# Batch 0's start in a fused attention and maxout kernel: q packed on VectorE and turned in whole blocks, the second k half in two column tiles, two row sums ahead of the first weight

## The chip, the cores and the metric

The kernel runs on one core of one Trainium2 chip. The time is the device time of an execution in microseconds (us), given as the median of several runs. A profiled execution gives a page (busy times, chain of waits, groups of instructions) and a trace that can be asked for single stretches. Engines are named as the profile names them: PE is TensorE (PEld its weight loads), DVE is VectorE, ACT is ScalarE, POOL is GpSimd, and SP issues transfers.

## The reference

Two computations follow each other: a Linformer attention and a feed-forward block with a maximum over three projections. Batch 8, 8 heads, sequence 1024, head size 64; k and v are projected along the sequence to 64 rows each.

```python
k_proj = np.einsum('ks,bhsd->bhkd', E, k)
v_proj = np.einsum('ks,bhsd->bhkd', F, v)
scores = scale * np.matmul(q, k_proj.transpose(0, 1, 3, 2))
attn = np.exp(scores - np.max(scores, axis=-1, keepdims=True))
attn = attn / (np.sum(attn, axis=-1, keepdims=True) + 1e-09)
attn_out = np.matmul(attn, v_proj)
x = attn_out.transpose(0, 2, 1, 3).reshape(8192, 512)
h = np.maximum(np.maximum(x @ w1, x @ w2), x @ w3)      # 512 -> 768
out = h @ w_out                                         # 768 -> 512
```

All inputs and the output are float32.

## The kernel before

Everything is computed in bfloat16 with float32 sums. The order of the instructions on each engine is written out by hand; PSUM is one tile of eight banks, and a small model of the engines' times (`clock`, `free`) picks at build time the bank that it takes to be free first (`bank()`, or `two()` for a pair of banks). The calls `at(...)` and `pe(...)` only move that model's time and make no instruction.

Heads are worked on in pairs (four pairs, 0 to 3), since two heads of 64 fill 128 partitions. A half of the sequence is 512 rows, four blocks of 128. For a pair and a half, the steps are: q is turned so that its head dimension lies on the partitions (`qTs`); k is projected with E and turned (`kpTs`); v is projected with F (`vps`); `scores` multiplies the turned q and k; `exps` takes the exponential on ScalarE; `sums` (called by `z(g)`) multiplies the exponentials by ones, and `invert` takes logarithm and exponential of the negative on ScalarE to get the reciprocal; `values` (called by `x(g)`) multiplies by v, and `scale_x` multiplies by the reciprocals on VectorE and writes xT, the input of the feed-forward block. The maximum of the scores is not subtracted.

Batch 0 has no earlier work to hide behind, so its start has code of its own, line by line in the order in which it stands:

- POOL issues all loads in one order, each casting to bfloat16: the first q half of heads 0 to 3, k of heads 0 to 3, the same of heads 4 to 7, v of pairs 0 and 1, two strips of w1, v of pairs 2 and 3, two more strips of w1, w2, w3 and the second q half, then `w_out` and batch 1. Up to eight are under way; a further one waits for the landing of the one eight places before.
- `turn_ef` turns E and F. `q_duo(u)` turns q of pairs 2u and 2u+1: 16 transposes of 128x64, straight from the loaded tile, whose two heads lie apart, into two row halves of a bank (`heads_q`), and one copy out on VectorE.
- `k_duo(u)` projects k of four heads in 8 matmuls of 256 columns with 64 output rows; `kt_duo(u)` turns the result in two transposes.
- `v_pair(g)` projects v of one pair in 8 matmuls.
- `idle(n)` issues matmuls on zeros, which keep TensorE busy while it waits for loads.
- After the hand-written sequence, `up_first` does the feed-forward matmuls of batch 0's first half. For w1 it runs over strips `ct` (128 rows of w1, so one pair of heads) and blocks `jt` (128 of the 768 columns): strip 0 and 1 for blocks 0 to 3, strip 0 and 1 for blocks 4 and 5, then strips 2 and 3. The rest of the attention is hung between these matmuls by a key (weight, strip, block), after which it runs. w2 and w3 follow, and in between the second half's q is packed on ScalarE (`pack_q`) and turned in 128x128 blocks (`qp`).

Later batches have their attention placed between the feed-forward matmuls of the batch before (`plan`).

Of the kernel before, what the change touches and what calls it, by code (L numbers as in the profile page):

```python
# [9 lines left out]
BF16 = mybir.dt.bfloat16  # L10
# [5 lines left out]
def kernel(  # L16
# [65 lines left out]
    def bank():  # L82
        n = min(range(8), key=lambda n: free[n])
        deal((n,))
        return psum_t[:, n, :], (n,)

    def pe(dt, wait=0.0):
        clock["pe"] = max(clock["pe"], wait) + dt
        return clock["pe"]
# [122 lines left out]
    def scores(b, g, lo, nsi):  # L212
        t, ns = two()
        n = nsi // 2
        for c in range(2):
            for hp in range(2):
                rows = slice(hp * HALF, (hp + 1) * HALF)
                at = g * SI + lo + c * n
                nc.tensor.matmul(  # L219
                    out=t[c * HALF:(c + 1) * HALF, hp, 0:n * P],  # L220
                    lhsT=k_pair(b, g)[rows],
                    rhs=qTs[b][rows, at:at + n, :],
                    start=True, stop=True,
                )
        return t[:, :, 0:n * P], ns, pe(n * MM / 4 + 0.1)

    def exps(b, g, lo, nsi, sc):
        t, ns, ready = sc
        pTs[b, g, lo] = att.tile([P, 2, CHUNK], BF16, name="pT", bufs=6)[:, :, 0:nsi * HALF]
        nc.scalar.activation(out=pTs[b, g, lo], in_=t, func=AF.Exp, scale=scale)  # L230
        runs("s", ready, 0.17 + nsi * 0.107, ns)
# [126 lines left out]
                )  # L358
        pe(8 * (width * 0.00042 + 0.01))

    def heads_q(b, g, sis, t):
        for i, si in enumerate(sis):
            for hp in range(2):
                nc.tensor.transpose(
                    out=t[hp * HALF:(hp + 1) * HALF, i * P:(i + 1) * P],
                    in_=qkv[b][0][:, 2 * g + hp, si, :],
                    identity=ident,
                )
        pe(0.08 * len(sis))

    q_pk = {}

    def pack_q(b, gs, lo, nsi):


        def f():
            if b not in q_pk:
                q_pk[b] = att.tile([P, NPAIR, SI, 2, D], BF16, name="q_p", bufs=1)
            for g in gs:
                copy(  # L380
                    "s", q_pk[b][:, g, lo:lo + nsi].rearrange("p si h d -> p h si d"),
                    qkv[b][0][:, 2 * g:2 * g + 2, lo:lo + nsi], (), 0.58,
                )
        return f
# [178 lines left out]
    def idle(n, w=warm):  # L563

        t, ns = bank()
        for _ in range(n):
            nc.tensor.matmul(out=t, lhsT=w[:, 0:P], rhs=w, start=True, stop=True)  # L567
        free[ns[0]] = pe(n * MM * (4 if w is warm_f else 1))
# [19 lines left out]
    def at(us):  # L588
        clock["pe"] = max(clock["pe"], us)
# [3 lines left out]
    def k_duo(u):  # L593
        t, ns = bank()
        for si in range(SI):
            nc.tensor.matmul(
                out=t[0:KP, 0:4 * D], lhsT=efT[:, si, 0:KP],
                rhs=k_t[:, 4 * u:4 * u + 4, si, :],
                start=(si == 0), stop=(si == SI - 1),
            )  # L600
        pe(0.9)
        kp0[u] = att.tile([KP, 4 * D], BF16, name="kp0")
        copy("v", kp0[u], t[0:KP, 0:4 * D], ns, 0.45)

    def kt_duo(u):
        t, ns = bank()
        t = t.bitcast(BF16)
        for gg in range(2):
            nc.tensor.transpose(
                out=t[:, gg * KP:(gg + 1) * KP],  # L610
                in_=kp0[u][:, gg * P:(gg + 1) * P], identity=ident[0:KP, 0:KP],
            )
        pe(0.15)
        copy(
            "v", kpTs[0][:, 2 * u:2 * u + 2, :].rearrange("a g k -> a (g k)"),
            t[:, 0:2 * KP], ns, 0.25,
        )

    def v_pair(g):
        t, ns = bank()  # L620
        for si in range(SI):
            nc.tensor.matmul(
                out=t[:, 0:2 * D], lhsT=efT[:, si, KP:3 * KP],
                rhs=v_t[:, 2 * g:2 * g + 2, si, :],
                start=(si == 0), stop=(si == SI - 1),
            )
        pe(0.5)
        copy(
            "v", vps[0][:, 2 * g:2 * g + 2].rearrange("a h d -> a (h d)"),
            t[:, 0:2 * D], ns, 0.3,  # L630
        )

    def q_duo(u):
        t, ns = bank()
        t = t.bitcast(BF16)
        for gg in range(2):
            heads_q(0, 2 * u + gg, range(SPC), t[:, gg * CHUNK:(gg + 1) * CHUNK])
        o = qTs[0].rearrange("a (g si) p -> a g si p", si=SI)
        copy(
            "v", o[:, 2 * u:2 * u + 2, 0:SPC, :],  # L640
            t.rearrange("a (g si p) -> a g si p", si=SPC, p=P), ns, 0.7,
        )
# [3 lines left out]
    def z(g):  # L646
        invert(0, g, *C0, sums(0, g, *C0))

    def x(g):
        scale_x(0, g, *C0, values(0, g, *C0))  # L650
# [16 lines left out]
    z(0)  # L667
    idle(1)
    z(1)
    idle(1)  # L670
    at(12.8)
    k_duo(1)
    idle(1)
    at(14.8)
    v_pair(0)
    kt_duo(1)
    x(0)
    for g in (2, 3):
        exps(0, g, *C0, scores(0, g, *C0))
    at(16.1)  # L680
    v_pair(1)
    at(17.4)

    ffn_sb = ctx.enter_context(tc.tile_pool(name="ffn_sb", bufs=2))
    hTs = {}
# [205 lines left out]
    for b in range(B):  # L891
        p = plan(b)

        def behind(ch, step):
            for f in p.get((ch, step), []):
                f()

        for ch in range(NCHUNK):
            if (b, ch) == (0, 0):
                c1 = (SPC, SPC)  # L900
                up_first({
                    (0, 0, 1): [lambda: x(1)],
                    (0, 0, 3): [lambda: z(2), lambda: z(3)],
                    (0, 1, 1): [lambda: v_pair(2)],
                    (0, 1, 3): [lambda: x(2)],
                    (0, 1, 5): [lambda: v_pair(3), ld(1)],
                    (0, 2, 1): [lambda: x(3)],
                    (2, "a", 0): [pack_q(0, (0, 1), *c1)],
                    (2, "a", 1): [pack_q(0, (2, 3), *c1)],
                    (2, "a", 3): [qp(0, (0, 1), *c1)],  # L910
                    (2, "a", 5): [qp(0, (2, 3), *c1)],
                    (2, 1): [duo[0].scores],
                    (2, 4): [
                        duo[0].sums, duo[0].values, duo[1].scores, duo[0].invert,
                    ],
                })
                run_later()
                behind(0, NJT - 1)
            else:
                for step in range(NJT):  # L920
                    up(b, ch, step, lambda: behind(ch, (step, "mid")))
                    behind(ch, step)
            for tt in range(SPC):
                down(b, ch, tt, "v" if b == 0 else "s")
                behind(ch, NJT + tt)
# [30 lines left out]
```

## Time and profile before

| | us |
|---|---|
| median of 5 runs | 399.05 (398.83 to 399.52) |
| profiled execution | 399.06 |
| its span, first to last instruction | 397.3 |
| TensorE busy | 387.4 (98%) |
| VectorE busy | 202.3 (51%) |
| ScalarE busy | 152.1 (38%) |
| granted TensorE clock, mean | 0.998 |
| HBM traffic over the span | 218 GB/s |

The page lists busy time by engine, the span in 40 slices (a digit is a tenth of busy time), the chain of work that ended last (followed back from the last instruction, at each step to what released it), and groups of instructions with what ended the idle time ahead of them. Lines of the timeline give start and length in us, engine, line of the kernel, operation, and what is written from what; x8 at the end is a number of instructions merged into the line, and the bracket tells how long the engine was idle before and what released it. Matmuls overlap, so a group's length holds the tail of its last one. Of the changed part: L364 are the transposes of `heads_q`, L596 `k_duo`, L609 `kt_duo`, L622 `v_pair`, L219 `scores`, L230 `exps`, L239 `sums` and `values`, L299 and L305 `invert`, L316 `scale_x`, L689 the w1 to w3 matmuls, L393 the transposes of `qp`, L567 `idle`, L102 every plain copy.

### The profile page before, as it was taken

To read this page: it belongs to the slowest core of one execution; us is meant where nothing else is said; L and a number is where in the kernel's file an instruction comes from. 1 tells how busy PE (TensorE), PEld (TensorE's weight loads), DVE (VectorE), ACT (ScalarE), POOL (GpSimd) and SP (SyncE) were. 2 spreads that over 40 slices of the span, in tenths; PEclk is the share of its full clock that TensorE was granted. 3 is DMA by queue.
4 is the path that set the end of the run, shared out by engine and by line. 5 is a ranking of instruction groups with operands and counts; after the bars stand their busy time and mean duration, and the time that the engine had idled before them with its cause. 6 is when DMAs were issued, how large, how long until landed. Compare 5 with 4: busy or idle time off the path is not lost.

```text
span 397.3 us, 5598 instructions
## 1 busy us (share of the span) xinstructions
PE 387.4 (98%) x2196; PEld 173.5 (44%) x2238; DVE 202.3 (51%) x309; ACT 152.1 (38%) x236; POOL 34.5 (9%) x49
## 2 busy tenths in 40 slices
PE   7899999999999999999999999999999999999996
PEld 3544443453445445444444444444444444444443
DVE  3348756751764525645374544845266443745251
ACT  2534638527222552263323532245323533132322
POOL 7450001000400200200002000200000000000000
PEclk9999999999999999999999999999999999999999
DMA  9999999987999998999979979696971138020202
GB/s 151 206 205 207 205 232 154 244 160 159 230 182 265 153 221 201 227 179 210 209 207 149 245 164 273 98 243 117 222 206 42 64 86 237 2 106 0 107 0 106
DMA packets 67338, 66.29 MB, mean 167 GB/s; under 512 B 31504, under 2 KB 59792, under 8 KB 67312
## 3 DMA queue, kind: packets, MB, share of 16 engines
q0 software_dynamic: 29104, 30.41, 47.7%
q1 hardware_dynamic: 38064, 35.46, 34.7%
q8 instruction: 17, 0.28, 0.3%
q10 hardware_dynamic: 144, 0.07, 0.1%
q14 instruction: 9, 0.07, 0.1%
HBM read 69.73 MB, written 16.97 MB: 218 GB/s over the span
## 4 chain that ended last, share of the span: by engine, by line
PE 89%; DMA 3%; DVE 2%; ACT 2%; issue 2%; POOL 2%; DVEq 0%; ACTq 0%; POOLq 0%
PE banks L689 60%; PE banks L797 20%; DMA v_t<-in_v_dram 3%; PE banks L353 2%; PE banks L239 2%; PE banks L219 2%; PE banks L528 1%; PE banks L264 1%; DVE xT L316 1%; ACT zl L299 1%; DVE m L758 1%; ACT zi_all L305 1%; DVE hT L699 0%; POOL k_t L152 0%; POOL q_t L157 0%
## 5 line engine op out<-in xcount | busy, mean ns | idle before, releaser
L689 PE MATMUL banks<-xT,w_sb 128*128 128x512 bf16 x1125 | 255.2, 379 | 1.9 <-DVE xT L316 0.3
L689 PEld LDWEIGHTS <-w_sb 128*128 128x128 bf16 x1152 | 110.1, 98 | 136.7 <-issue 8.4
L758 DVE TENSOR_TENSOR m<-banks,h1s 128x512 f32<-128x512 f32 x90 | 62.1, 690 | 131.1 <-ACT h1s L754 88.5
L754 ACT COPY h1s<-banks 128x512 f32<-128x512 f32 x90 | 52.7, 586 | 119.5 <-PE banks L689 119.5
L797 PE MATMUL banks<-wout_sb,hT 128*128 128x512 bf16 x364 | 85.5, 379 | 1.0 <-issue 0.3
L699 DVE TENSOR_TENSOR hT<-banks,m 128x512 bf16<-128x512 f32 x90 | 62.3, 692 | 9.7 <-DVE m L758 0.5
L797 PEld LDWEIGHTS <-hT 128*128 128x128 bf16 x378 | 35.3, 98 | 48.4 <-issue 6.1
L102 ACT COPY o_sb<-banks 128x512 f32<-128x512 f32 (+2 forms) x57 | 32.9, 578 | 58.3 <-PE banks L797 50.6
L316 DVE TENSOR_TENSOR xT<-banks,zi_all 128x1024 bf16<-128x1024 f32 x28 | 33.2, 1220 | 12.8 <-PE banks L239 8.2
L230 ACT ACTIVATE pT<-banks 128x1024 bf16<-128x1024 f32 (+1 forms) x32 | 30.2, 975 | 15.9 <-PE banks L219 15.9
L201 POOL DMA_DIRECT2D q_t<-in_q_dram x7 | 6.2, 880 | 196.7 <-DMA qT<-q_p 85.0
L102 ACT CAST vp<-banks 64x256 bf16<-64x256 f32 (+1 forms) x11 | 4.7, 424 | 20.5 <-DVE kp L102 11.2
L102 DVE CAST vp<-banks 64x256 bf16<-64x256 f32 (+2 forms) x15 | 6.7, 444 | 10.1 <-ACT vp L102 7.3
L239 PE MATMUL banks<-pT,vp 64*64 64x512 bf16 (+1 forms) x128 | 10.3, 375 | 0.5 <-DVE vp L102 0.2
L102 DVE COPY q_p<-q_t 128x1024 bf16<-128x1024 bf16 x26 | 9.7, 434 | 0.4 <-DMA q_t<-in_q_dram 0.4
L219 PE MATMUL banks<-qT,kpT 64*64 64x512 bf16 (+1 forms) x128 | 9.7, 372 | 0.0
L102 DVE CAST kp<-banks 128x256 bf16<-128x256 f32 (+2 forms) x9 | 4.6, 509 | 8.5 <-PE banks L528 3.5
L102 DVE COPY o_sb<-banks 128x512 f32<-128x512 f32 (+1 forms) x9 | 5.6, 640 | 5.4 <-PE banks L777 4.5
L567 PE MATMUL banks<-warm_f 128*128 128x512 f32 x8 | 6.6, 971 | 1.5 <-DVE warm_f L175 1.5
L299 ACT ACTIVATE zl<-banks 128x512 f32<-128x512 f32 (+1 forms) x8 | 6.5, 811 | 2.9 <-PE banks L239 2.7
L353 PEld LDWEIGHTS <-efT 128*64 128x64 bf16 x128 | 6.6, 110 | 2.1 <-issue 2.1
L201 POOL DMA_DIRECT2D v_t<-in_v_dram x7 | 6.5, 930 | 1.0 <-PE banks L689 1.0
(76 smaller groups left out, 136.3 us busy)
## 6 DMA issues: line engine op xcount, KB each, us to landing
out_dram<-o_sb SPq DMA_DIRECT2D x30, 512.0 KB, 3.9
zi_all<-zd SPq DMA_DIRECT2D x20, 512.0 KB, 8.0
q_t<-in_q_dram POOLq DMA_DIRECT2D x7, 1024.0 KB, 10.2
k_t<-in_k_dram POOLq DMA_DIRECT2D x7, 1024.0 KB, 16.5
v_t<-in_v_dram POOLq DMA_DIRECT2D x7, 1024.0 KB, 21.5
zi_all<-zd POOLq DMA_DIRECT2D x4, 512.0 KB, 7.5
w_sb<-in_moe_w_dram POOLq DMA_DIRECT2D x4, 384.0 KB, 11.0
k_t<-in_k_dram POOLq DMA_DIRECT2D x2, 512.0 KB, 9.1
```

The lines of the kernel that those rows point to most:

```text
L102: done = {"v": nc.vector.tensor_copy, "s": nc.scalar.copy, "g": nc.gpsimd.tensor_copy}[eng](out=o, in_=i)
L201: dma = nc.gpsimd.dma_start(out=tiles[i], in_=view((q, k, v)[i], b))
L219: nc.tensor.matmul(out=t[c * HALF:(c + 1) * HALF, hp, 0:n * P], lhsT=k_pair(b, g)[rows], rhs=qTs[b][rows, at:at + n, :], start=True, stop= ...
L230: nc.scalar.activation(out=pTs[b, g, lo], in_=t, func=AF.Exp, scale=scale)
L239: nc.tensor.matmul(out=t[hp * HALF:(hp + 1) * HALF, c, 0:nsi * HALF], lhsT=w(rows, hp), rhs=p[rows, hp, :], start=True, stop=True,)
L316: nc.vector.tensor_tensor(out=xTs[b][:, g, lo:lo + nsi, :].rearrange("a (c s) p -> a c (s p)", c=2), in0=t, in1=zi, op=ALU.mult,)
L353: nc.tensor.matmul(out=t[hh * HALF:(hh + 1) * HALF, 0:width], lhsT=efT[:, si, (kv - 1) * KP:kv * KP], rhs=qkv[b][kv][:, heads[hh], si, :], ...
L689: nc.tensor.matmul(out=h, lhsT=w_sb[i][:, ct, jt * P:(jt + 1) * P], rhs=xTs[b][:, ct, ch * SPC:(ch + 1) * SPC, :], start=(ct == first), st ...
L699: nc.vector.tensor_tensor(out=o, in0=h, in1=other, op=ALU.max)
L754: nc.scalar.copy(out=h1s, in_=h[0][0])
L758: nc.vector.tensor_tensor(out=m12, in0=h[1][0], in1=h1s, op=ALU.max)
L797: nc.tensor.matmul(out=o_ps, lhsT=hTs[b, ch][:, jt, tt * P:(tt + 1) * P], rhs=wout_sb[:, jt, :], start=(jt == 0), stop=(jt == NJT - 1),)
```

## The change

Four things change, all in the start of batch 0; the loads and their order stay.

- `q_duo` first packs its pairs of q on VectorE (`pack_q`, which had ScalarE as its only engine), so that the two heads of a pair lie side by side, and turns 8 blocks of 128x128 in place of 16 of 128x64. `heads_q` goes.
- The second half of k is projected by `k_quad`: heads 4 and 5 into output rows 0 to 63, heads 6 and 7 into rows 64 to 127, as two column tiles of the array, 16 matmuls of 128 columns (`proj`, L353 before). `kt_quad` turns the result in one transpose. Two `idle(1)` go and one is moved.
- Scores of pairs 2 and 3 come ahead of `x(0)`, and their sums `z(2)`, `z(3)` ahead of the first w1 matmul; they stood behind w1's strip 0, block 3.
- `v_pair(2)` moves from behind strip 1, block 1 to behind strip 1, block 3, and `x(2)` from there to behind strip 0, block 5.

```diff
-    def heads_q(b, g, sis, t):
-        for i, si in enumerate(sis):
-            for hp in range(2):
-                nc.tensor.transpose(
-                    out=t[hp * HALF:(hp + 1) * HALF, i * P:(i + 1) * P],
-                    in_=qkv[b][0][:, 2 * g + hp, si, :],
-                    identity=ident,
-                )
-        pe(0.08 * len(sis))
...
-    def pack_q(b, gs, lo, nsi):
+    def pack_q(b, gs, lo, nsi, eng="s"):
...
                 copy(
-                    "s", q_pk[b][:, g, lo:lo + nsi].rearrange("p si h d -> p h si d"),
+                    eng, q_pk[b][:, g, lo:lo + nsi].rearrange("p si h d -> p h si d"),
...
+    def k_quad(u):
+
+        t, ns = bank()
+        proj(0, 1, t, (slice(4 * u, 4 * u + 2), slice(4 * u + 2, 4 * u + 4)), 2 * D)
+        kp0[u] = att.tile([P, 2 * D], BF16, name="kp0q", bufs=1)
+        copy("v", kp0[u], t[:, 0:2 * D], ns, 0.27)
+
+    def kt_quad(u):
+        t, ns = bank()
+        t = t.bitcast(BF16)
+        nc.tensor.transpose(out=t[:, 0:P], in_=kp0[u], identity=ident)
+        pe(0.1)
+        copy(
+            "v", kpTs[0][:, 2 * u:2 * u + 2, :].rearrange("a g k -> a (g k)"),
+            t[:, 0:P], ns, 0.25,
+        )
...
     def q_duo(u):
+        pack_q(0, (2 * u, 2 * u + 1), 0, SPC, "v")()
         t, ns = bank()
         t = t.bitcast(BF16)
         for gg in range(2):
-            heads_q(0, 2 * u + gg, range(SPC), t[:, gg * CHUNK:(gg + 1) * CHUNK])
+            for si in range(SPC):
+                at = (gg * SPC + si) * P
+                nc.tensor.transpose(
+                    out=t[:, at:at + P],
+                    in_=q_pk[0][:, 2 * u + gg, si].rearrange("p h d -> p (h d)"),
+                    identity=ident,
+                )
+        pe(0.5)
...
     z(1)
+    at(12.8)
+    k_quad(1)
     idle(1)
-    at(12.8)
-    k_duo(1)
-    idle(1)
+    kt_quad(1)
     at(14.8)
     v_pair(0)
-    kt_duo(1)
-    x(0)
     for g in (2, 3):
         exps(0, g, *C0, scores(0, g, *C0))
+    x(0)
     at(16.1)
     v_pair(1)
-    at(17.4)
+    z(2)
+    z(3)
+    at(17.0)
...
                     (0, 0, 1): [lambda: x(1)],
-                    (0, 0, 3): [lambda: z(2), lambda: z(3)],
-                    (0, 1, 1): [lambda: v_pair(2)],
-                    (0, 1, 3): [lambda: x(2)],
+                    (0, 1, 3): [lambda: v_pair(2)],
+                    (0, 0, 5): [lambda: x(2)],
                     (0, 1, 5): [lambda: v_pair(3), ld(1)],
```

## The prediction

> **What bounds the kernel now.** I read the page first, then the chain of waits, the waits of the start, and the timeline from 7 to 36 us.
>
> ```profile
> span 397.3 us, 5598 instructions
> PE 387.4 (98%) x2196; PEld 173.5 (44%) x2238; DVE 202.3 (51%) x309; ACT 152.1 (38%) x236; POOL 34.5 (9%) x49
> DMA  9999999987999998999979979696971138020202
> PE banks L689 60%; PE banks L797 20%; DMA v_t<-in_v_dram 3%; PE banks L353 2%; PE banks L239 2%; PE banks L219 2%; PE banks L528 1%; PE banks L264 1%; DVE xT L316 1%; ACT zl L299 1%; DVE m L758 1%; ACT zi_all L305 1%; DVE hT L699 0%; POOL k_t L152 0%; POOL q_t L157 0%
> ```
>
> TensorE is on the chain nearly everywhere, but the DMA row is full from the first slice, and the chain holds one transfer, v_t. The chain of the first 36 us in order of time shows where:
>
> ```profile
> 7.47 12.86 DMA v_t<-in_v_dram
> 20.33 0.05 issue
> 20.37 0.62 PE banks L622 x8
> 20.99 0.43 PE banks L689 x2
> 21.43 0.02 issue
> 21.45 0.30 PE banks L239 x4
> 21.75 0.97 PE banks L689 x4
> 22.72 0.50 PE banks L622 x8
> ```
>
> The third v transfer (pair 2) is issued at 7.47 and lands at 20.33; the projection of pair 2 (L622) starts 0.05 later. So before 20.33 TensorE cannot set the end, and what it does there is priced at nothing unless it is late for a landing. The landings, from the DMA view (issue plus time to landing): first q half 6.58, first k half 10.00, second q half 11.38, second k half 13.88, v pairs 0 and 1 at 15.16 and 16.45, w1's strips 17.43, 19.45, 22.56, 23.51, v pairs 2 and 3 at 20.33 and 21.65, w2 25.40 and 27.32, w3's first half 29.16, the q of sequence half 2 at 31.82, w3's second half 33.70. These issues wait only for earlier landings, the instruction order on POOL is unchanged, so the landings stay.
>
> After 20.33, in the timeline:
>
> ```profile
> 20.83 0.59 PE L689 MATMUL banks<-xT,w_sb 128*128 128x512 bf16 x2
> 21.10 0.29 DVE L102 CAST vp<-banks 128x128 bf16<-128x128 f32 x1 [1.74 <-PE banks L622]
> 21.45 0.30 PE L239 MATMUL banks<-pT,vp 64*64 64x256 bf16 x4
> 21.87 0.69 DVE L316 TENSOR_TENSOR xT<-banks,zi 128x512 bf16<-128x512 f32 x1 [0.48 <-PE banks L239]
> 22.61 0.61 PE L622 MATMUL banks<-v_t,efT 128*128 128x128 bf16 x8
> 31.84 2.18 ACT L102 COPY q_p<-q_t 128x512 bf16<-128x512 bf16 x4 [5.09 <-DMA q_t<-in_q_dram]
> ```
>
> The reader is to see a serial chain: project pair 2, cast it (VectorE), apply it, scale it (VectorE, until 22.56), and only then project pair 3 at 22.61. The four w1 matmuls before that end their issue at 22.55, so TensorE waits 0.06 for the scale, whose PSUM bank pair 3 reuses. The last line is the next DMA-bound point: ScalarE's packs of q start with their landing.
>
> **The change, part by part.** The profiled execution took 399.06 us (span 397.3, 1.76 around it), 0.01 over the median 399.05.
>
> First half of q, before k lands. Removed: 16 transposes and loads of 64 columns, 7.33 to 7.96 (issue 0.57 us). Added: two VectorE copies of 512 columns and 8 transposes of 128x128. A copy: the trace has 128x512 SBUF to SBUF at 0.283 (efT), 128x1024 at 0.42 (q_p); I take 0.28 with a start every 0.2, bounds 0.2 to 0.42. They stand behind VectorE's first efT copy (7.43 to 7.86) and end near 8.3. The transposes (0.056 apart in the q_p group on L393: 0.61 for 8) then end near 8.75, the following fp32 warm-up matmul (issue 1.12) near 9.8. The first k projection waits for its landing at 10.00 and starts at 10.04 in both: cover 0.24 us. What waits behind the copies on VectorE (the qT copy, 0.69, and the efT copy, 0.28) ends near 9.7, before its users at 12.13 and 15.2. Cost nothing.
>
> Second half of q. Its two copies follow the kpT copy (11.85 to 12.07) and end near 12.5; TensorE has scores until 12.47. The second four transposes start near 12.55 instead of 12.68, and the whole ends where it did, near 13.1, 0.05 either way. Sums of pair 0 wait for ScalarE's exponential (13.08) anyway. Cost nothing.
>
> A collision is possible in both places, since POOL issues transfers at 7.47 to 8.20 and 11.67 to 12.21. The trace has one q_p copy during such an issue:
>
> ```profile
> L102 DVE COPY q_p<-q_t x26: 407/421/791, 43.2 to 277.8; 128x1024 bf16<-128x1024 bf16 x26
> 103.12 1.15 POOL L201 DMA_DIRECT2D v_t<-in_v_dram  x1
> 86.43 0.88 POOL L201 DMA_DIRECT2D q_t<-in_q_dram  x1 [25.12 <-DMA qT<-q_p]
> ```
>
> The slowest copy (791 instead of 421 ns) started at 103.70, inside a POOL issue of 1.15 instead of 0.88. So a collision costs VectorE 0.37 and POOL 0.27. With 0.37 the first k projection would start 0.13 late (0.37 less its cover 0.24), and that is swallowed at 19.45 as below. The 0.27 at POOL falls on an issue whose transfer lands 12.86 later behind full queues: bounds 0 and 0.27 on the landing, I take 0 (DMA rates are 205 to 208 GB/s all through).
> The Trainium skill, "SBUF — State Buffer", section "Who interferes with whom", speaks against this part: a VectorE copy in a two-port mode shuts GpSimd out of SBUF for its whole length, and POOL-issued transfers need GpSimd for their descriptors. By that rule the sum would carry an estimate of 0.3 us on pair 2's landing, 399.3; by the rows it carries nothing.
>
> Second half of k. Removed: one 128x512 warm-up (0.22), 8 matmuls of 256 columns (14.24 to 15.30), a 64x256 cast of 0.416 that began at 15.41 because it waited for ScalarE, two 64-column transposes, one warm-up. Added: 16 matmuls of 128 columns in two column tiles, one cast 128x128 (0.29, the vp row), a warm-up, one transpose. The landing (13.88) releases it at 13.95. The row of L353, also two column tiles, has a pair each 0.109 at 256 columns; the 64-column q transposes have a pair each 0.053 at 128. I take 0.055: 8 pairs 0.44; upper bound 0.87, as if the shorter stream saved nothing. Cast 14.6 to 14.9, transpose to 15.15, kpT copy to 15.45. Scores 2, 3 then start after pair 0's projection (landing 15.16, issue 15.2 to 15.65) at 15.66 instead of 16.59. Their exponentials wait for ScalarE's inversion of pair 1 (ends 16.03) and run from 16.0 to 17.1 instead of 16.94 to 18.03. A gain of 0.93 locally.
>
> Pairs 2, 3's sums ahead of w1. They move from 19.01 to about 16.95 and 17.35; the latter waits for pair 0's scale, whose PSUM bank it takes. The first w1 matmul comes near 17.6 to 17.7 (before 17.72: its strip landed at 17.43). Then 2 w1, pair 1 applied, 2 more w1, done at 18.7. Here the gain ends: next in TensorE's order are four matmuls of w1's second strip, which lands at 19.45. TensorE stands about 0.8 us. So up to 0.8 us of lateness in all the steps above is free too.
>
> Pair 2's projection, now behind all four matmuls of the second strip (before: two, with two after). They start at 19.45 + 0.046 (landing to matmul, as 20.328 to 20.374 for v) = 19.49; 4 x 0.216 = 0.864 ends their issue at 20.36. Pair 2's landing releases it at 20.374. Cost: nothing, by a margin of 0.02 us. Its cast no longer waits for ScalarE as well: before it began 0.106 after the matmuls' end (20.994), other vp casts 0.04; gain 0.065. Apply at 21.38 (the two w1 matmuls ahead end at 21.26), scale ends 22.50, two w1 matmuls between, pair 3 at 22.55 instead of 22.61. TensorE now stands 0.4 us there, where it stood 0.06: the rest of the gain goes here.
>
> From there on the order on every engine is that of before, with the PSUM banks renamed throughout. The one added wait, batch 2's q load on VectorE's copies of 12.5, stands at 58.68 and is long fulfilled; SP's queue is unchanged. The strips of w1 (22.56, 23.51) and w2 (25.40; used from 26.07) lie earlier than their use.
>
> Sum: 399.06 - 0.065 + 0 = 399.0. Of roughly 1 us that TensorE saves, the landings and the scale give 0.065.
> The Trainium skill, "TensorEngine Tiling (Array Packing)", section "Restrictions", adds that column tiling turns fast weight loading off; the L353 loads (16 in 0.80) hold that in the upper bound of 0.87 already, and by the rule the sum would still be 399.0.
>
> **The rivals.** About 0.2%, 0.8 us, is what a measurement of this kernel tells from no change.
> A, slower: w1's second strip lands nearer to pair 2 than 0.88 us. Four matmuls now stand between that landing and pair 2's projection, so each 0.1 us closer costs 0.1. For it: the margin is 0.02, and neighbouring landings lie 0.88 to 2.02 apart. Against it: the issues are unchanged. Landing together costs 0.86: 399.06 - 0.065 + 0.86 = 399.85.
> B, more gain: the chain through pair 2 is shorter than I think, and TensorE reaches ScalarE's packs of q early. These follow the landing at 31.82: the second ends at 32.98, and the second four transposes, at 33.19 before, cannot start before 33.02. That caps the gain at 0.17: 398.9.
> C, slower: VectorE's copies, at 0.79 each, delay the first k projection by about 1 us (2 x 0.79 less 0.48 is 1.1 late, less the cover 0.24, so 0.86). The stand at 19.45 absorbs 0.8: 399.1. It decides only beyond 0.8.
> D, slower: TensorE's clock falls as it idles more. It stood 1.02 us before the first k projection and the granted clock read 1.00 after; the new stands are 0.8 and 0.4. Half clock for the 7 w1 matmuls or so of one stand would cost 7 x 0.216 = 1.5: 400.5.
>
> **How the numbers follow.** Forecast 0.72, B 0.10, A 0.11, C 0.04, D 0.03. The predicted time is 399.0. Low: the lowest run 398.83 less B's 0.17, rounded down, 398.6; high: A's end, 399.85. That leaves out D and part of the runs' own scatter (398.83 to 399.52). Beyond 0.8 us: slower D, a third of A, a little of C and 0.02 for causes that I do not see, 0.10; faster only by an unseen cause, since B is capped, 0.07; within, 0.83.
>
> **What would show it.** Right: scores of pairs 2, 3 near 15.7, TensorE standing before 19.45 and again before pair 3's projection, which starts at 22.5 to 22.6; the q_p transposes from 32.9. Wrong: pair 2's projection clearly after its landing (A), new VectorE copies above 0.5 us (C), w1 matmuls more than 0.216 apart (D), or landings that moved, above all those of w1's second strip and v pair 2.

## The result and the profile after

The changed kernel takes 399.69 us (median of 23 runs, 399.03 to 400.86), the kernel before 399.13 in the same comparison (42 runs, 398.57 to 399.95): ratio 1.0015, 95% interval 1.0009 to 1.0021. It is slower by 0.6 us. That lies inside the range given and under the 0.2% that I had named as the limit of what can be told, but so many runs tell more, and "no change" was the wrong call.

The profiled execution took 399.48 us. From its page, the span, TensorE's row, the DMA row of the 40 slices and the chain by line:

```profile
span 397.7 us, 5581 instructions
PE 386.5 (97%) x2186; PEld 173.2 (44%) x2228; DVE 203.0 (51%) x313; ACT 151.9 (38%) x236; POOL 34.2 (9%) x49
DMA  8999999988999999999978969796970138020202
PE banks L705 58%; PE banks L813 19%; DMA qT<-q_p 3%; PE banks L239 2%; PE banks L219 2%; DMA k_t<-in_k_dram 2%; PE banks L353 2%; PE banks L518 1%; DVE xT L316 1%; PE banks L264 1%; DVE m L774 1%; PE banks L629 1%; ACT zi_all L305 1%; ACT zl L299 1%; DVE hT L715 0%
```

TensorE works 0.9 us less and the span is 0.4 longer. The chain held v_t before; it no longer does. A new transfer stands in its place, `qT<-q_p`, which the prediction never mentions: the DMA transpose of batch 1's q.

The chain of the changed kernel in order of time (start, length, what), around the place that had the wait for v pair 2:

```profile
18.66 0.04 issue
18.70 0.70 DVE xT L316
19.40 0.04 issue
19.45 1.02 PE banks L705 x4
20.47 0.45 PE banks L629 x8
20.92 0.43 PE banks L705 x2
21.35 0.28 PE banks L239 x4
...
22.47 0.61 PE banks L629 x8
```

Pair 2's projection (now L629) starts at 20.31 behind four w1 matmuls (now L705), which wait for pair 1's scale; v pair 3 starts at 22.47, where it was 22.61. The start is 0.14 us ahead, and so is everything up to 56.6 us. Then, still in the chain:

```profile
41.13 2.67 PE banks L813 x12
43.80 13.10 DMA qT<-q_p
56.90 0.14 issue
57.03 0.63 PE banks L219 x8
```

The transpose was issued at 43.80 and landed at 56.90; batch 1's scores (L219) wait for it and start at 57.03, 0.43 later than before (56.60, landing 56.40). From there to the end the difference stays 0.43, which is the 0.42 between the two profiled executions.

What the DMA engines do just ahead of that landing, from the DMA view of 54.4 to 56.4 us, first the changed kernel, then the one before; the third view is the kernel before from 51 to 53 us (a column of the rows is 0.05 us):

```profile
DMA  9999999999991190000000011010001010010105
GB/s 604 271 256 237 276 256 282 256 282 215 61 46 36 36 26 0 0 0 0 0 0 0 0 10 10 5 10 5 10 5 10 10 10 10 10 10 5 15 5 128
q1 hardware_dynamic: 634, 0.15, 119.1%
q8 instruction: 1, 0.02, 3.6%
```

```profile
DMA  2999819991929999999999999999999991399999
q1 hardware_dynamic: 1565, 0.39, 120.9%
q0 software_dynamic: 9, 0.01, 2.2%
```

```profile
DMA  9999999989798979799999999799999992999911
GB/s 215 195 215 189 174 230 143 266 133 261 123 261 138 297 138 292 148 553 190 210 179 169 184 184 190 169 195 164 154 118 113 51 41 46 31 46 31 5 5 20
q8 instruction: 1, 0.02, 3.0%
```

The transpose's 256-byte packets (q1) nearly stop for 1.5 us in the changed kernel, and one packet of another kind is in the window, an instruction fetch of 16 KB (q8), at 54.4. Before, that packet came at 51.9, and there too the transpose nearly stopped soon after, from 52.6 to 53.7 us: the stop is not new, it lies nearer to the landing. There are 17 such packets in a run. "Runtime: NRT & Kernel Launch" of the Trainium skill, section "Instruction fetch mechanics", says that an engine's instructions are refilled in blocks of 256, 16 KB each, over a DMA queue of its own. The profile of before records 4444 instructions of TensorE, 17.4 blocks of 256, so the trace agrees. The change takes 20 instructions from TensorE in the first 17 us (32 fewer in q's transposes and their loads, 16 more in k's projection, 4 fewer in k's turn and a warm-up; in all one `idle(1)` goes, not two as the list of the change has it), so each later block is reached that much later. The page calls the cost of such a fetch mostly hidden. TensorE has no idle time beside the one at 54.4 here either, but in the two kernels' profiles such a packet held a DMA engine for 0.88 to 1.45 us.

That gave three theories: the place of the instruction fetches among the transfers (T1), the new order of the instructions (T2), scatter of the landings whatever the kernel (T3). The runs then moved T1 from the transpose to the loads of the start; from e9 on the expectations call the loss at v pair 2's load theory A and the loss at the transpose theory B.

### The profile page after: what moved, and what is told of

Its sections match the earlier page's. It is cut to its first block, busy times and chain, and to the rows that moved or that the text cites. A ratio compares the mean times of both kernels' runs of the same rounds, so it can differ in the third digit from the quotient of the medians.

```text
span 397.7 us, 5581 instructions
## 1 busy us (share of the span) xinstructions
PE 386.5 (97%) x2186; PEld 173.2 (44%) x2228; DVE 203.0 (51%) x313; ACT 151.9 (38%) x236; POOL 34.2 (9%) x49
## 4 chain that ended last, share of the span: by engine, by line
PE 88%; DMA 5%; DVE 3%; issue 2%; ACT 1%; POOL 0%; DVEq 0%; ACTq 0%; POOLq 0%
PE banks L705 58%; PE banks L813 19%; DMA qT<-q_p 3%; PE banks L239 2%; PE banks L219 2%; DMA k_t<-in_k_dram 2%; PE banks L353 2%; PE banks L518 1%; DVE xT L316 1%; PE banks L264 1%; DVE m L774 1%; PE banks L629 1%; ACT zi_all L305 1%; ACT zl L299 1%; DVE hT L715 0%
## 5 line engine op out<-in xcount | busy, mean ns | idle before, releaser
L705 PE MATMUL banks<-xT,w_sb 128*128 128x512 bf16 x1125 | 255.2, 379 | 2.0 <-DVE xT L316 0.5
L705 PEld LDWEIGHTS <-w_sb 128*128 128x128 bf16 x1152 | 110.3, 98 | 137.1 <-issue 9.1
L770 ACT COPY h1s<-banks 128x512 f32<-128x512 f32 x90 | 52.6, 585 | 119.6 <-PE banks L705 119.6
L102 DVE COPY q_p<-q_t 128x1024 bf16<-128x1024 bf16 (+1 forms) x30 | 10.8, 420 | 0.0
L219 PE MATMUL banks<-qT,kpT 64*64 64x512 bf16 (+1 forms) x128 | 9.7, 371 | 0.5 <-DMA qT<-q_p 0.5
L353 PEld LDWEIGHTS <-efT 128*64 128x64 bf16 x144 | 7.1, 110 | 2.2 <-issue 2.1
```

Source lines behind the costliest of these rows:

```text
L102: done = {"v": nc.vector.tensor_copy, "s": nc.scalar.copy, "g": nc.gpsimd.tensor_copy}[eng](out=o, in_=i)
L219: nc.tensor.matmul(out=t[c * HALF:(c + 1) * HALF, hp, 0:n * P], lhsT=k_pair(b, g)[rows], rhs=qTs[b][rows, at:at + n, :], start=True, stop= ...
L353: nc.tensor.matmul(out=t[hh * HALF:(hh + 1) * HALF, 0:width], lhsT=efT[:, si, (kv - 1) * KP:kv * KP], rhs=qkv[b][kv][:, heads[hh], si, :], ...
L705: nc.tensor.matmul(out=h, lhsT=w_sb[i][:, ct, jt * P:(jt + 1) * P], rhs=xTs[b][:, ct, ch * SPC:(ch + 1) * SPC, :], start=(ct == first), st ...
L770: nc.scalar.copy(out=h1s, in_=h[0][0])
```

## The experiments

One reading holds for all of them. In each of the 18 profiled executions (both kernels, 16 runs), the time is 399.06 plus the amount by which batch 1's scores start later than 56.60, within 0.04 us. The scores start 33.99 after v pair 3, or later where something makes them wait. So two numbers of a profile hold all of its difference: the start of v pair 3 and a wait ahead of batch 1's scores. The table has twelve of them; the others stand with their runs.

| profiled execution | TensorE instructions against before | first, third fetch | v pair 2 landed | v pair 3 starts | transposed q landed | scores wait | time |
|---|---|---|---|---|---|---|---|
| before | 0 | 17.4, 51.9 | 20.33 | 22.61 | 56.40 | 0 | 399.06 |
| changed | -20 | 19.1, 54.4 | 19.76 | 22.47 | 56.90 | 0.58 | 399.48 |
| e1 | 0 | 17.5, 51.5 | 20.00 | 22.20 | 55.98 | 0 | 398.63 |
| e3 | -30 | 18.7, 54.6 | 20.70 | 22.90 | 56.78 | 0.02 | 399.41 |
| e4 | 0 | 17.2, 51.5 | 20.02 | 22.71 | 56.05 | 0 | 399.17 |
| e5 | -20 | 19.0, 54.8 | 20.98 | 23.18 | 57.01 | 0 | 399.62 |
| e6 | -18 | 18.5, 54.5 | 20.61 | 22.89 | 57.03 | 0.29 | 399.61 |
| e7 | 0 | 17.7, 52.1 | 20.10 | 22.31 | 56.06 | 0 | 398.76 |
| e8 | -12 | 18.9, 53.1 | 20.91 | 23.20 | 56.92 | 0 | 399.66 |
| e12 | -20, 0 from 26 us | 18.4, 51.6 | 19.23 | 21.93 | 55.66 | 1.04 (elsewhere) | 399.45 |
| e14 | +2 | 18.0, 51.5 | 20.08 | 22.37 | 55.88 | 0 | 398.78 |
| e15 | 0 | 17.8, 52.0 | 20.80 | 23.09 | 56.58 | 0 | 399.55 |

### Put the count back, take more away, or change the order alone

e1: the changed kernel with ten small matmuls on zeros (20 TensorE instructions with their loads) in the first warm-up. "Ten small matmuls" below is this edit.

```diff
         for _ in range(n):
             nc.tensor.matmul(out=t, lhsT=w[:, 0:P], rhs=w, start=True, stop=True)
+        if w is warm_f and n == 3:
+            for _ in range(10):
+                nc.tensor.matmul(
+                    out=t[:, 0:16], lhsT=warm[:, 0:P], rhs=warm[:, 0:16],
+                    start=True, stop=True,
+                )
```

> Edit: the changed kernel with 10 small matmuls of 16 columns on zeros (20 TensorE instructions) behind the first warm-up, where TensorE waits for E and F to be cast. Theory 1 (place of the instruction fetch): the changed kernel has about 20 TensorE instructions fewer ahead of 50 us, so the 16 KB instruction fetch of before's 51.9 us comes at 54.4, in the DMA transpose of batch 1's q, which pauses for 1.5 us and lands at 56.9 instead of 56.4; TensorE waits 0.5 for it. With the 20 instructions back, the fetch is near 51.9, the transpose lands near 56.3, scores of batch 1 start near 56.4 to 56.5, time 399.0, 0.1 under before. Theory 2 (the change itself, its order or its earlier landings, makes the transpose late): the count does not matter, 399.7, 0.5 over before. Theory 3 (the transposes scatter whatever the kernel): nothing to do with either, 399.1 to 399.7 with no wait at a fixed place.

Measured: 399.10, ratio to before 1.0004 (0.9994 to 1.0015). The fetch is back at 51.5, the transpose landed at 55.98, no wait. With 20 instructions added that do no work, the ratio is 1.0004 and not 1.0015; how much of the loss is gone, the intervals leave open.

e2: the same, with the first fp32 warm-up as bf16 matmuls.

```diff
+        if w is warm_f and n == 3:
+            for _ in range(24):
+                nc.tensor.matmul(out=t, lhsT=warm[:, 0:P], rhs=warm, start=True, stop=True)
...
```

> Edit: as the run with 20, and the first fp32 warm-up (3 matmuls of 4 passes) is given as 24 bf16 matmuls of the same length, together some 56 TensorE instructions more than the changed kernel. Theory 1: the fetch comes at 48 to 48.5, when loads still fill the queues and the transpose has hardly begun; the transpose lands at 55.5 to 56.4, scores of batch 1 start at 56.4 to 56.5, time 399.0. Theory 2: 399.7.

Measured: 400.79, 1.0045 (1.0031 to 1.0060). It tells nothing of the count: the 24 matmuls took 8.23 us, not the length of the fp32 ones (they start 0.43 apart until 7.26 us and 0.216 apart, as w1's, from 7.65 on), so the q transposes began at 11.47 and not 8.31, and v pair 3 at 25.07.

e3: the changed kernel without its bf16 warm-ups.

```diff
-        for _ in range(n):
+        for _ in range(n if w is warm_f else 0):
```

> Edit: the changed kernel without its five bf16 warm-up matmuls (10 TensorE instructions fewer). Theory 1: the fetch comes near 55.6; without a pause the transpose would land near 55.4, so either it is through (399.0) or its last packets pause (57 to 57.3, time 399.9 to 400.2). Theory 2: 399.7. A slower TensorE clock without warm-ups would show in the starts before 20 us.

Measured: 399.42, 1.0006 (0.9994 to 1.0018). The profile is late by 0.29 at v pair 3, whose chain starts with v pair 2's load (landed 20.70); there is no wait at the scores. So a loss can sit wholly in the start, which T1 as I had it does not say.

e4: the kernel before with the new order alone.

```diff
-    x(0)
     for g in (2, 3):
         exps(0, g, *C0, scores(0, g, *C0))
+    x(0)
     at(16.1)
     v_pair(1)
+    z(2)
+    z(3)
...
-                    (0, 0, 3): [lambda: z(2), lambda: z(3)],
-                    (0, 1, 1): [lambda: v_pair(2)],
-                    (0, 1, 3): [lambda: x(2)],
+                    (0, 1, 3): [lambda: v_pair(2)],
+                    (0, 0, 5): [lambda: x(2)],
```

> Edit: before, with the order alone of the change (scores of pairs 2, 3 ahead of x(0), their sums ahead of w1, projection and application of v pair 2 later); no instruction more or fewer. Theory 1: fetch near 51.9 and transposes as before, 399.0 to 399.1, within 0.1 of before. Theory 2, if the order is the cause: 399.7.

Measured: 399.46, 1.0010 (1.0001 to 1.0019). At the count of the kernel before, the order alone cost 0.0010; with the earlier steps shortened too and the count restored (e1) no such loss shows. The profiled execution (399.17) is one of the faster ones and holds 0.1 us of it, in this chain:

```profile
18.95 0.70 DVE xT L316
19.65 0.04 issue
19.69 1.02 PE banks L691 x4
20.71 0.45 PE banks L622 x8
```

Pair 1's scale ends at 19.65, the four matmuls follow, and pair 2's projection starts at 20.55, 0.5 behind its load (20.02).

### The changed kernel again, and three pairs for the count

e5 is the changed kernel, no edit.

> The changed kernel once more, nothing left out. Fetch theory (fewer TensorE instructions put a 16 KB instruction fetch at 54.4 us, beside the DMA transpose of batch 1's q, which then lands late): the fetch again near 54.4, the transpose again stalled until about 56.4 and landed near 56.9, a wait of about 0.5 us ahead of batch 1's scores, whose start lies 0.3 to 0.5 later than the start of v pair 3 would put it. Order theory (the four matmuls of the second k-half strip now ahead of v pair 2 wait for x(1)'s scale): v pair 2 starts within 0.1 of the later of (end of x(1)'s scale + 0.92) and (landing of v pair 2's load + 0.05). Both hold at once: 399.4 to 399.9. If the wait at batch 1's scores is absent here, the fetch theory loses its place as the cause and the profile of the result was one draw.

Measured: 399.68, 1.0016 (1.0007 to 1.0025), the result repeated. But the profile is late in another place: v pair 2 landed at 20.98, v pair 3 started at 23.18, and the transposed q (57.01) was in time.

```profile
7.58 13.41 DMA v_t<-in_v_dram
20.98 0.04 issue
21.02 0.61 PE banks L629 x8
```

Here the wait at batch 1's scores is absent: as the expectation said, the fetch beside the transpose loses its place as the cause.

e6: the new q and k parts under the old order.

```diff
...
     z(1)
+    idle(1)
     at(12.8)
     k_quad(1)
     idle(1)
-    kt_quad(1)
     at(14.8)
     v_pair(0)
+    kt_quad(1)
+    x(0)
     for g in (2, 3):
         exps(0, g, *C0, scores(0, g, *C0))
-    x(0)
...
-    z(2)
-    z(3)
...
-                    (0, 1, 3): [lambda: v_pair(2)],
-                    (0, 0, 5): [lambda: x(2)],
+                    (0, 0, 3): [lambda: z(2), lambda: z(3)],
+                    (0, 1, 1): [lambda: v_pair(2)],
+                    (0, 1, 3): [lambda: x(2)],
```

> The kernel before with the new q packs, 128-wide q turns and the second k half in two column tiles, but with the old order of sums, x(0) and v pair 2. It has nearly the changed kernel's count of TensorE instructions. Fetch theory: the fetch near 54, the transposed q of batch 1 landed 56.7 to 57.0, a wait of 0.2 to 0.5 at batch 1's scores; time 399.2 to 399.5 against 399.0 for the kernel before. Order theory: no part of the loss is here, so the start of v pair 3 at 22.2 to 22.6 and the time at or under the kernel before, 398.7 to 399.0.

Measured: 399.59, 1.0010 (1.0002 to 1.0019); 0.28 late at v pair 3, behind a load that landed at 20.61, and 0.29 of wait at the scores. The order theory, which had no loss here, falls as the whole cause.

e7: e1 with v pair 2 and x(2) at their old places.

```diff
-                    (0, 1, 3): [lambda: v_pair(2)],
-                    (0, 0, 5): [lambda: x(2)],
+                    (0, 1, 1): [lambda: v_pair(2)],
+                    (0, 1, 3): [lambda: x(2)],
```

> The changed kernel with ten 16-column matmuls on zeros behind the first warm-up (so that the count of TensorE instructions is that of the kernel before) and with v pair 2 and x(2) back at their old places in the w1 order, two matmuls of the second strip ahead of v pair 2 and not four. If both causes are right, the fetch lies near 51.5, batch 1's scores do not wait, and the time is 398.7 to 399.0, at or 0.1 under the kernel before, and 0.1 to 0.4 under the same kernel with the new place (399.10). If the place of v pair 2 costs nothing, this comes out with that one, 399.0 to 399.2. If scatter of the landings is all, anything between 398.9 and 399.5 with no wait that tells them apart.

Measured: 399.10, 1.0003 (0.9994 to 1.0012), as e1: with the count restored, the place of v pair 2 doesn't show.

e8: the kernel before without its bf16 warm-ups, 12 instructions fewer; the edit is that of e3.

> The kernel before without its bf16 warm-up matmuls on zeros (12 TensorE instructions fewer, nothing of the computation). Fetch theory: the fetch near 53.3, the transposed q of batch 1 landed later than 56.40, a wait of 0 to 0.4 at batch 1's scores; time 399.0 to 399.4. Order theory: start phase as before unless the clock of TensorE starts lower, time 398.8 to 399.1. The changed kernel without the same warm-ups showed no lower clock and started v pair 3 only by its load's landing.

Measured: 399.42, 1.0010 (1.0001 to 1.0019). So the kernel before can be made slower in this way too; again it is v pair 2's load (20.91) and not the transpose.

e14 and e15 close the pairs. e14 is e6 with the ten small matmuls:

> The new q packs and turns and the second k half in two column tiles under the old order (399.59, ratio 1.0010), with ten 16-column matmuls on zeros behind the first warm-up: the count of TensorE instructions is the kernel before's to within 2 rows. Count theory: the fetches at 17.1 to 17.8 and 51.5 to 52.1, v pair 2's load landed by 20.4, no wait at batch 1's scores, 398.8 to 399.1, 0.3 to 0.7 under the same kernel without the matmuls. If the count is not the cause: 399.4 to 399.7 as without them.

Measured: 399.30, 1.0005 (0.9996 to 1.0014), 0.2 over the expected window and 0.29 under e6. e15 keeps e8's count by making those warm-ups 16 columns wide:

```diff
-            nc.tensor.matmul(out=t, lhsT=w[:, 0:P], rhs=w, start=True, stop=True)
+            m = CHUNK if w is warm_f else 16
+            nc.tensor.matmul(
+                out=t[:, 0:m], lhsT=w[:, 0:P], rhs=w[:, 0:m], start=True, stop=True
+            )
```

> The kernel before with its six bf16 warm-up matmuls on zeros 16 columns wide and not 512: the work is gone, the count of TensorE instructions stays. Count theory: as the kernel before, 398.9 to 399.2, fetches at 17.1 to 17.8 and 51.5 to 52.1. If it was the missing warm-up work that made the same kernel without these instructions slower (399.42, ratio 1.0010): 399.3 to 399.6.

Measured: 399.10, 1.0001 (0.9993 to 1.0010). It was not the warm-up work that e8 missed. The profiled execution is the slowest of the eleven (399.55; v pair 2 landed at 20.80 there), so single profiles scatter as much as the effect is large.

### Move the two waits themselves

e9: the first transpose issued earlier, by packing its q in the 0.8 us that VectorE stands at 39.7.

```diff
+                (0, 5): [qd(1, range(2))],
                 (0, 6): [
...
-                    qd(1, range(2)), duo[1].scale, qd(1, range(2, 4), "s"), store_now,
+                    duo[1].scale, qd(1, range(2, 4), "s"), store_now,
```

> The changed kernel with the packs of batch 1's first two q pairs one step earlier on VectorE (into the 0.8 us that it stands at 39.7), so that the first DMA transpose of batch 1's q is issued near 40.6 and not at 43.8 to 44.5. Theory A (the loss is the landing of v pair 2, which the first instruction fetch now hits): start of v pair 3 at 22.5 to 23.2 as in the changed kernel, carried 1:1 to the end; no wait at batch 1's scores; 399.4 to 399.7, at most 0.2 better than the changed kernel. Theory B (the loss is the late transpose): the wait goes and with it the loss, 398.9 to 399.2.

Measured: 400.85, 1.0042 (1.0030 to 1.0054), wrong under both theories. I had overlooked what the pack itself waits for. Its waits from 39 to 45 us:

```profile
DVE q_p L102 <- DMA q_t<-in_q_dram: 2.3, 1, 2.3
PEld L813 <- issue: 1.8, 3, 1.4
PE banks L813 <- DVE o_sb L102: 1.1, 1, 1.1
```

Batch 1's q lands at 42.63. VectorE stood before the pack, with the PSUM copies behind it, and TensorE waited 1.1 for those: 1.23 lost. The run says nothing of the theories, only that the transposes can't be issued earlier without an earlier load.

e10: v pair 2's load and projection ahead of w1's second strip.

```diff
-    load_w(0, slice(1, 2))
     load_kv(2, V2)
+    load_w(0, slice(1, 2))
...
-                    (0, 1, 3): [lambda: v_pair(2)],
-                    (0, 0, 5): [lambda: x(2)],
+                    (0, 0, 3): [lambda: v_pair(2)],
+                    (0, 1, 1): [lambda: x(2)],
```

> The changed kernel with the load of v pair 2 issued ahead of w1's second strip, v pair 2 behind the four matmuls of the first strip and x(2) behind the second matmul of the second strip. Theory A: v pair 2's load lands near 18.5 to 19.5, its projection starts by 19.6 and not at 20.3 to 21.0, v pair 3 starts at 21.6 to 22.2 and is then bound by its own load (21.4 to 21.8). What follows is ahead by 0.5 to 1.0 until batch 1's scores, and there most of it is lost: the transposed q lands at 56.5 to 57.0 whatever TensorE does, so a wait of 0.4 to 1.0 opens at the scores. 399.1 to 399.5. If the start phase doesn't matter, 399.6 to 399.8 with no new wait.

Measured: 399.43, 1.0011 (1.0002 to 1.0019). The time is as expected, the way is not. V pair 2 landed at 18.66 and started at 19.29, but the second strip, now behind it, landed at 20.87:

```profile
7.74 13.13 DMA w_sb<-in_moe_w_dram
20.87 0.04 issue
20.91 0.61 PE banks L705 x2
```

The lateness stays with the position in the queue and not with the tensor: v pair 2, third behind v pairs 0 and 1 in the changed kernel, lands near 20.9 when it is late, and so does the strip in its place.

e11: e10, e9 and the ten small matmuls together.

> Both edits together (v pair 2's load ahead of w1's second strip with v pair 2 and x(2) earlier; the first DMA transpose of batch 1's q issued some 3 us earlier), and ten 16-column matmuls on zeros behind the first warm-up, so that the fetches lie where the kernel before has them. Theory A and the transpose as the next bound: v pair 3 at 21.6 to 22.1, no wait at batch 1's scores, their start 0.5 to 0.9 ahead of the kernel before (56.60), carried to the end: 398.1 to 398.6, ratio 0.998 to 0.999. If batch 1's scores then wait for another load or the w strips of the start phase land too late, less than half of it.

Measured: 400.88, 1.0063 (1.0043 to 1.0082), spoilt by e9's wait as above. The start is of use: v pair 3 at 22.12, 0.49 ahead of before, with the second strip at 20.00.

e12: the ten small matmuls behind w1's last matmul and not in the warm-up.

```diff
                     (0, 2, 1): [lambda: x(3)],
+                    (0, 3, 5): [lambda: pad(10)],
```

> The changed kernel with the ten 16-column matmuls on zeros not in the warm-up but behind the last w1 matmul of batch 0's first chunk (near 26 us; at most 0.3 us of TensorE). The first fetch stays near 19, the third goes back to 51.5 to 52.1. Theory A: start of v pair 3 as in the changed kernel, 22.5 to 23.2, and with it 399.4 to 399.9. Theory B: the transposed q of batch 1 lands at 56.0 to 56.4 and not at 56.8 to 57.0, no wait at the scores; 399.1 to 399.4 with the 0.3 of the matmuls in it.

Measured: 400.20, 1.0026 (1.0017 to 1.0035). The time can't be used: a new wait of about 1 us opens near 38, most likely because the matmuls take a PSUM bank of their own and the planner's later banks shift:

```profile
37.14 0.37 PE banks L451 x8
37.51 0.03 ACTq L462
37.54 0.04 issue
37.58 1.03 ACT zl L462
38.62 0.04 issue
38.66 0.41 PE banks L434 x8
```

One part bears on the transpose all the same: with the third fetch back at 51.6, the transpose issued at 44.29 landed at 55.66; in the changed kernel it was issued at 43.80 and landed at 56.90. In the start of this profile v pair 2 landed at 19.23 although the first fetch was late (18.4), against theory A.

e13 and e16: e10's loads, with all six matmuls of w1's first strip ahead of v pair 2; e13 has the ten small matmuls, e16 not.

```diff
-            (0, range(0, 4)), (1, range(0, 4)), (0, range(4, 6)), (1, range(4, 6)),
-            (2, jts), (3, jts),
+            (0, jts), (1, jts), (2, jts), (3, jts),
...
-                    (0, 0, 3): [lambda: v_pair(2)],
-                    (0, 1, 1): [lambda: x(2)],
+                    (0, 0, 5): [lambda: v_pair(2)],
+                    (0, 1, 2): [lambda: x(2)],
```

> The changed kernel with the load of v pair 2 ahead of w1's second strip, all six matmuls of the first strip ahead of v pair 2 and the second strip's six behind it (x(2) behind their third), and ten 16-column matmuls on zeros behind the first warm-up; the transposes of q stay. Theory: v pair 2 starts at 19.4 to 19.6 (20.37 before), v pair 3 at 21.7 to 22.1 (22.61 before), all later work 0.5 to 0.9 ahead until batch 1's scores, where the transposed q (landed 56.0 in the three padded runs) leaves 0.0 to 0.3 of wait: 398.3 to 398.7, ratio 0.998 to 0.9995. If the start phase is not bound by that load: 399.0 to 399.2.

> The same as the one with v pair 2's load ahead and the first strip's six matmuls first, without the ten small matmuls: the fetch falls at 18.4 to 19.1. Count theory: the fetch hits w1's second strip, now behind v pair 2 (landed 20.0 with the matmuls, 20.9 without them), and the second strip's matmuls wait for it: v pair 3 at 22.3 to 22.9, batch 1's q transposed by 56.6 to 57.0; 399.0 to 399.5, 0.4 to 0.8 over the run with the matmuls. If the count is not the cause: as that run, within 0.2.

Measured: e13 399.00, 0.9998 (0.9989 to 1.0007); e16 399.31, 1.0010 (1.0001 to 1.0019). e16 came as expected (v pair 3 at 22.66, transposed q at 56.95). In e13 the start did what it should (v pair 2 at 19.53, v pair 3 at 21.88, 0.73 ahead of before), and nearly all of that was lost again in one place:

```profile
40.61 2.86 PE banks L818 x13
43.47 12.91 DMA qT<-q_p
56.38 0.14 issue
56.52 0.63 PE banks L219 x8
```

A wait of 0.65 at batch 1's scores, where I had allowed 0.3. This is the best version found. It is not faster than the kernel before, and none of the runs is.

### What the runs say together

Four pairs of kernels differ by TensorE instructions that compute nothing. Ratios to the kernel before, with fewer instructions and with the count restored:

| pair | fewer | restored | difference |
|---|---|---|---|
| changed (e5), e1 | 1.0016 | 1.0004 | 0.0012 |
| e6, e14 | 1.0010 | 1.0005 | 0.0005 |
| e8, e15 | 1.0010 | 1.0001 | 0.0009 |
| e16, e13 | 1.0010 | 0.9998 | 0.0012 |

Each ratio is known to about 0.0009 either way, and three of the pairs were measured on different chips, each kernel beside the kernel before on its own; e16 and e13 ran side by side. All four differences have the same sign. Their mean is 0.00095, about 0.0005 either way by the scatter of the runs (pairs share runs of the kernel before): 0.4 us. This part is shown: with 12 to 20 TensorE instructions fewer early in the program, under both orders of the work and both orders of the loads, the kernel is slower than with the count made up.

It is not a law of the count alone. e3, with 30 fewer, lost no more (1.0006) than those with 12 to 20 fewer, and e4 lost 0.0010 at the count of before. Nor are the small matmuls quite nothing, since they take TensorE about 0.3 us at the start (6.74 to 7.05 in e1). But e15 has less work there than the kernel before, with the same count, and the same time.

How it comes about is read from the profiles and less sure. The transposed q landed at 55.66 to 56.58 in the eight executions whose third fetch lies at 51.5 to 52.1 and at 56.61 to 57.03 in the seven where it lies at 53.1 to 54.8, with no overlap (e2 left out for its late start, e9 and e11 for their moved pack). But the second group was also issued 0.3 us later on average (44.23 against 43.91), and from issue to landing the groups overlap (11.37 to 12.91 and 12.29 to 13.10), so part of that is the late start. V pair 2, in the old load order, landed at 20.22 on average in six executions with the first fetch at 17.2 to 18.0, and at 20.45 in seven with it at 18.4 to 19.1; five of those seven lie at 20.6 to 21.0 (e9 is one of them) and two at 19.2 and 19.8, so the groups overlap. Where the second strip stands in its place, it landed at 19.98 and 20.00 with the ten small matmuls (e13, e11) and at 20.77 and 20.87 without (e16, e10). No run moves a fetch without changing the count. That the fetch itself delays these transfers therefore stays an inference from its place; what is shown is the effect of the count.

Of the 0.0015 of the result, some 0.001 goes with the count. The rest, 1.0004 (0.9994 to 1.0015) with the count restored, is not told from nothing.

## Why the prediction was wrong

What held, by its own steps:

- The q packs cost nothing. The two copies ended at 8.44 (8.3 forecast) and the transposes at 8.93 (8.75), and the first k projection was released at 10.18 (10.04) by nothing but its landing, 10.14. The timeline of the changed kernel:

```profile
7.40 0.73 POOL L152 DMA_DIRECT2D v_t<-in_v_dram  x1
7.89 0.55 DVE L102 COPY q_p<-q_t 128x512 bf16<-128x512 bf16 x2
8.31 0.62 PE L647 MATMUL banks<-ident,q_p 128*128 128x128 bf16 x8 [0.79 <-DVE q_p L102]
10.18 0.49 PE L586 MATMUL banks<-k_t,efT 128*64 128x256 bf16 x3 [0.34 <-DMA k_t<-in_k_dram]
```

- The collision with POOL (0.37 and 0.27 in the trace of before) did not show. The first copy of each two overlapped an issue of POOL (v pair 2's, 7.40 to 8.13, and a w1 strip's, 11.77 to 12.31). Two copies together took 0.55 and 0.49, the issues 0.73 and 0.54 as before, and v pair 2's load landed earlier, not later, in this execution. No cost shows here of the kind that the rule of the Trainium skill ("SBUF — State Buffer", section "Who interferes with whom") would have given this part. Rival C is out.
- K's second half: cast from 14.75 to 15.04 (14.6 to 14.9 forecast), scores of pairs 2 and 3 at 15.88 (15.66); the local gain is 0.71 for 0.93. The sums came at 17.16 and 17.50 (16.95, 17.35).
- V pair 2 started at 20.31 (20.374) and v pair 3 at 22.47 (22.55). The gain of the start is 0.14 for 0.065. The order of TensorE from there on is that of before.
- The granted clock stayed at 1.0, so D is out. Rival B's cap was not reached.

What failed, in the prediction's words: "These issues wait only for earlier landings, the instruction order on POOL is unchanged, so the landings stay." They do not. The second strip of w1, on which the four matmuls were to start at 19.49, landed at 18.49; they started at 19.45 because pair 1's scale ended then, so a right number came out for another reason. V pair 2 landed at 19.76 in one execution of the changed kernel and 20.98 in the next. Its margin of 0.02 us had no meaning beside that scatter, and where v pair 2 lands late, v pair 3 is late with it and the end too, 1:1.

The second failure follows from it: "From there on the order on every engine is that of before". True, and not enough. I stopped at 36 us and took the same order for the same time. But in the profile of before the transposed q of batch 1 landed 0.2 us ahead of its use (56.40, scores at 56.60), and the order of the instructions does not fix that landing. In the profiled execution it was 0.50 late there and cost 0.58 against what the start allowed.

The sum also lacks a term: 20 TensorE instructions fewer were priced as TensorE time alone. With the count put back, the forecast of "no change" fits (1.0004 and, at the old place of v pair 2, 1.0003). The size of the missing term is 0.4 us by the four pairs; that it acts through these two landings is read from the profiles and not shown.

Rival A had the right sign and the right victim (v pair 2), and its end of 399.85 holds the time, but its mechanism was not seen: the second strip landed 1.27 ahead of v pair 2 and not closer than 0.88. Where the order alone was changed (e4), what the four matmuls waited for was pair 1's scale, a wait that I had called free.

## What to carry to other kernels

Landings read from one profiled execution are one draw: before a margin of 0.02 or 0.2 us decides a forecast, look at more than one execution, and follow every tight landing to the end of the program, not only to the end of the edit. When a change removes or adds instructions on an engine, ask where its instruction fetches fall afterwards; a control with as many small instructions on zeros tells the effect of the count apart from that of the change itself. Where loads bound the start, a saving in front of them is returned at the next landing: e13 gained 0.73 us there and gave 0.65 back at a transpose.

## What the runs showed of the hardware that I had not expected

- The count of TensorE instructions early in the program moves the time by about 0.4 us in the four pairs, without any change in the computation. That this comes about by where the 16 KB instruction packets (0.88 to 1.45 us each on a DMA engine) fall among the loads is inferred, not shown.
- A DMA transpose in packets of 256 bytes all but stops for some 1.6 us: the packets that are held (most others take 0.02 us) span 52.05 to 53.74 before and 54.86 to 56.42 in the changed kernel, in both within 0.5 us of a fetch. A later transpose has such a stall with no fetch within 5 us (80.54 to 81.98 before, 81.05 to 82.62 in the changed kernel), so the fetch is not the only thing that can cause one.
- Twenty-four bf16 matmuls on zeros at the program's start (e2) start 0.43 us apart until 7.26 us, 5.5 us after the first, and 0.216 apart from 7.65 on, the pace of w1's matmuls of the same width. The granted clock in the profile's rows reads 1.00 over both stretches.
